# A list scheduler's weights for weights transfers are changed, and the order of a fused GateLoop and SwiGLU kernel is made anew

## The chip, the cores and the metric

The kernel runs on one core of a Trainium2 chip. The time is device microseconds of one execution; the median of three runs before the change is 721.65 us (721.41 to 721.87).

## The reference

Four batches of eight heads run a gated linear recurrence over 768 steps with head size 48. Its result, laid out as 3072 tokens of 384 features, goes through an RMS norm and a SwiGLU feed-forward with 1536 hidden features. The four weights come as 64-bit floats, the rest as 32-bit floats.

```
mag = sqrt(a_re*a_re + a_im*a_im);  scale = minimum(mag, 0.999) / (mag + 1e-06)
for t in range(S):
    new_re = ar * S_re - ai * S_im
    new_im = ar * S_im + ai * S_re
    S_re, S_im = (new_re + einsum('bhd,bhe->bhde', k[t], v[t]), new_im)
    y[t] = einsum('bhd,bhde->bhe', q[t], S_re)
x = y as (batch*time, heads*dim);  xn = x / sqrt(mean(x*x) + 1e-06) * rms_g
g = xn @ w_gate;  out = (g * sigmoid(g) * (xn @ w_val)) @ w_out
```

## The kernel before

**Tiling.** Time is cut into chunks of 128 steps, 24 in all (six for each batch). Gates are computed for units: chunks 0 and 1 alone (units 0 and 1), then pairs. `load_gates` and `load_kq` bring `a_re`, `a_im`, `q` and `k` of a unit; `gates` computes, with products along time on VectorE (`scan`), how much each feature has decayed and turned up to each step, and multiplies `q` and `k` by the cosine and sine of the turn. The results are the rotated rows, `rot`. Six transfers for each chunk move them into the layout by heads, `kq`; in the code they are `moved[n]`, in the profile `kq<-rot`.

`attend(n)` does a chunk: scores (`bank<-kq`, 64 small matmuls whose first operands are parts of `kq`), masking with `COPY_PREDICATED` into `am`, transposes of the keys (`bank<-ident,kq`, copied to `kt` by ScalarE), output (`bank<-am,ve` and `bank<-kq,state`), the new state (`bank<-vn,kt`, then an addition and a product by the decay on VectorE), and the norm: squares on ScalarE (`sq`), their column sum on TensorE (`bank<-ones,sq`), `ssv` on VectorE, the power -0.5 on GpSimd (`rs`, the "root" row), its broadcast over columns (`bank<-ident,rs` for early chunks, through two GpSimd transfers for most later ones), and the normed input `xT` on VectorE.

`feed(g, xT)` does the feed-forward of two chunks. It runs twelve blocks of six matmuls with a moving width of 256, by turns `bank<-xT,wg` and `bank<-xT,wv`; ScalarE takes `Silu` of one into `sg`, and VectorE multiplies by the other into `hT`. Then comes the product with `wo`: for groups 0 and 1 six blocks of four matmuls (`bank<-wo,hT` 128x384), for later groups in a form with seven half-products and sums.

**Weights.** The 64-bit weights are brought in twelve pieces: six of 1536 KB for `w_gate` and `w_val`, and six of 768 KB for `w_out`, all from GpSimd's queue. `fetch` places each raw piece in `wo` or `hT`, which are not needed yet, and after it issues a one-element copy on GpSimd (`junk`) that waits for the landing. From the third piece on a transfer waits for the landing of the one two before it. The last `w_gate` piece (the sixth transfer) is also held until the rows of chunk 1 have landed (`cleared`; the copies `seen` wait for the rows of chunks 0 and 1). The transfers go out in the order 1, 0, 3, 2, 5, 4 of `pieces`, `w_val` ahead of `w_gate`. `narrow` turns a raw piece into 32 bits: an `Activation` on ScalarE, and on VectorE a shift (`TENSOR_SCALAR`), a bit step (`SCALAR_TENSOR_TENSOR`) and an addition (`CUSTOM_DVE_ANT_0`). The same weights are looked at once more later, from SP's queue (`look`), to check their range.

**What sets the order.** Nothing in the loops. Every operation is first recorded by `add` with an assumed duration and, for transfers, an assumed load and packet weight. `dates` goes back from the due times of the feed-forward's blocks to a due time for each operation, and adds `flow.shift[stage, index]`, a table found by a search. `schedule` then plays the list forward: at each moment an engine takes, of its ready operations, the one that is due first. Transfers in flight at once share by their packet weights. `issue` writes the instructions in the order that results. On the chip each engine works strictly in this order and waits on semaphores, so an order that was good under wrong assumptions shows as waiting. SP has eight transfers under way at most: the ninth waits for the first to land. Where the planner sees TensorE idle early on, it puts warm-up matmuls (`bank<-rot` 128x128, `flow.warm`) into the order.

The lines to follow are `dma` (its `load` and `packet`), `flow.shift`, and in the profile line 676, from which all operations are issued, so that groups are told apart by their tiles.

Of the kernel before, what the change touches and what calls it, by code (L numbers as in the profile page):

```python
# [461 lines left out]
class Flow:  # L462
# [9 lines left out]
    turn = 0.0  # L472
# [50 lines left out]
    def add(self, eng, calls, dur, reads=(), writes=(), table=None, land=None, due=None, after=(), behind=(), late=None, mode=None, group=None):  # L523
        op = dict(i=len(self.ops), eng=eng, calls=calls, dur=dur, deps=set(), table=table, land=land,
                  base=due, late=late, mode=mode, group=group, stage=self.stage, behind={o["i"] for o in behind})
        self.ops.append(op)
        op["deps"].update(o["i"] for o in after)
        for ap in reads:
            self.note(op, ap, False)
        for ap in writes:  # L530
            self.note(op, ap, True)
        return op
# [146 lines left out]
def fast(tc, ctx, qT, kT, v, a_re, a_im, w_gate, w_val, w_out, rms_g, out, H, bad):  # L679
# [27 lines left out]
    def room(name, shape, dtype=FP32):  # L707
        t = mem.tile(shape, dtype, name=name, tag=name)
        row = 1
        for x in shape[1:]:  # L710
            row *= x
        rooms[t.tensor.name] = (name, row * mybir.dt.size(dtype))
        keep.append(t)
        return t
# [72 lines left out]
    def run(x):  # L787
        n = 1
        for step, size in reversed([tuple(y) for y in x.ap][0 if x.tensor.name in outside else 1:]):
            if step != n:  # L790
                break
            n *= size
        return n

    def dma(o, x, eng="SP", slow=0.0, **kw):
        n = mybir.dt.size(o.dtype)
        for s in o.shape:
            n *= s
        row = mybir.dt.size(o.dtype) * min(run(o), run(x))
        load = n / row * (0.006 + 50.3e-6 * row) / 16  # L800
        op = add(eng, [(QUEUE[eng].dma_start, (), dict(out=o, in_=x))], 0.85 if eng == "POOL" else 0.62, [x], [o],
                 land=2.0 + 1.4 * load + slow, **kw)
        op["slow"] = slow
        op["load"] = load
        op["packet"] = max(0.07, 0.006 + 50.3e-6 * row * (2 if eng == "POOL" and row == 2048 else 1))
        return op

    def mms(list_, dur, **kw):
# [53 lines left out]
    row = room("row", [P, C])  # L862
# [31 lines left out]
    for o, order in ((band, "p (x h) -> p x h"), (head, "p (x h) -> p h x")):  # L894
        add("DVE", [(nc.vector.tensor_reduce, (), dict(out=o, in_=ident.rearrange(order, h=H), axis=mybir.AxisListType.X,
                                                       op=ALU.add))], 0.3, [ident], [o], late=LATE)
    for r in range(ND):
        o = pick[:, r].rearrange("p (x j) -> p x j", j=2 * ND)[:, :, r::ND]
        copy(o, band.unsqueeze(2).to_broadcast([P, P // H, 2]), late=LATE)
    dma(gcol, rms_g.rearrange("(c p) -> p c", p=P))  # L900


# [21 lines left out]
    def fetch(i, piece, raw, eng):  # L924
        to, ap, c, f = piece
        rows, n = to.shape[1:]
        src = ap.bitcast(I32).rearrange("(c p) f -> p c f", p=P)[:, c, 2 * f:2 * (f + n)]
        raw3 = raw.rearrange("p (c f) -> p c f", c=rows)
        if eng == "POOL" and i >= AHEAD:
            wait = [landed[i - AHEAD]]  # L930
        elif eng == "POOL":
            wait = [begun[0]]
        else:
            wait = []
        if eng == "POOL" and i in CLEAR:
            wait = wait + [cleared[CLEAR[i]]]
        sent = dma(raw3, src, eng, after=wait)
        if eng == "POOL":
            landed[i] = add("POOL", [(nc.gpsimd.tensor_copy, (), dict(out=junk, in_=raw[0:1, 1:2]))], 0.8,
                            after=[sent])  # L940
        words = raw.rearrange("p (n two) -> p n two", two=2)
        return words[:, :, 0], words[:, :, 1]
# [3 lines left out]
    def narrow(i):  # L946
        flow.stage = "w", i
        to, ap, c, f = pieces[i]
        rows, n = to.shape[1:]
        if ap.dtype == FP32:  # L950
            dma(to, ap.rearrange("(c p) f -> p c f", p=P)[:, c, f:f + n], "POOL")
            return
        lo, hi = (x.rearrange("p (c f) -> p c f", f=n) for x in fetch(i, pieces[i], places[i], "POOL"))
        t = to.bitcast(I32)
        act(lo, lo.bitcast(U32), AF.Copy, scale=2.0 ** -29)
        step = n // 2 if i in HALVED else n
        for f in range(0, n, step):
            to_, lo_, hi_ = (x[:, :, f:f + step] for x in (t, lo, hi))
            add("DVE", [(nc.vector.tensor_scalar, (),
                         dict(out=to_, in0=hi_, scalar1=3, scalar2=None, op0=ALU.logical_shift_left))],  # L960
                0.15 + 0.52e-3 * rows * step, [hi_], [to_])
            stt(to_, hi_, 0x3FFFFFFF, to_, ALU.bitwise_or, ALU.bitwise_and)
            tt(to_, to_, lo_, ALU.add)
# [22 lines left out]
    turn = {}  # L986
# [381 lines left out]
    for in_, limit, op in ((ef, P_MIN, ALU.is_ge), (ef, 1.0, ALU.is_le), (range_, 0.0, ALU.is_le),  # L1368
# [15 lines left out]
    flow.warm = dict(after=started, until=WARM, call=[  # L1384
        (nc.tensor.matmul, (banks[3][:, 0:C],), dict(lhsT=filler[:, 0:C], rhs=filler[:, C:2 * C], start=True, stop=True))])
    flow.shift = {
        ("attend", 0): -38.4, ("attend", 1): -1.9, ("attend", 2): -16.2, ("attend", 3): -0.7,
        ("attend", 4): -35.7, ("attend", 6): -12.2, ("attend", 11): -3.9, ("attend", 18): 6.0,
        ("attend", 19): -5.7, ("attend", 20): -1.5, ("attend", 21): 11.1, ("attend", 22): 4.2, ("feed", 4): 7.5,
        ("feed", 7): 1.6, ("feed", 8): 4.4, ("feed", 9): 16.9, ("feed", 11): -26.3, ("kq", 2): -10.9,  # L1390
        ("kq", 6): -3.3, ("kq", 7): -15.8, ("kq", 9): 8.6, ("load", 1): -4.5, ("load", 2): -33.3,
        ("load", 3): 50.7, ("load", 11): -5.2, ("load", 12): -6.8, ("norm", 0): -0.8, ("norm", 1): -5.1,
        ("norm", 5): -4.6, ("norm", 16): 4.4, ("norm", 20): 1.8, ("norm", 21): -20.2, ("norm", 22): -8.0,
        ("root", 1): -1.3, ("root", 2): -5.7, ("root", 3): 41.8, ("root", 5): 2.8, ("root", 9): 9.4,
        ("rot", 1): -4.3, ("rot", 2): 0.4, ("rot", 3): -2.6, ("rot", 5): 10.3, ("rot", 10): -10.2,
        ("rot", 12): 4.7, ("size", 2): -2.7, ("size", 3): 14.9, ("size", 7): -0.3, ("size", 10): 14.6,
        ("size", 11): 53.4, ("size", 12): 18.6, ("state", 0): 20.7, ("state", 1): -6.7, ("state", 2): -18.1,
        ("state", 3): -5.4, ("state", 4): -2.1, ("state", 10): 0.2, ("state", 14): -4.9, ("state", 20): -17.7,
        ("turn", 0): -5.1, ("turn", 1): -18.8, ("turn", 4): 7.1, ("turn", 5): 47.3, ("turn", 6): -2.5,
        ("turn", 8): -28.6, ("turn", 9): 0.3, ("turn", 11): -2.5, ("w", 0): -2.6, ("w", 3): -20.3, ("w", 5): -3.8,  # L1400
        ("w", 6): -7.5, ("w", 10): -31.1, ("y", 0): -12.7, ("y", 1): -1.0, ("y", 7): 1.7, ("y", 10): 4.5,
        ("y", 11): -0.4, ("y", 15): 0.8, ("y", 17): -2.8, ("y", 20): 2.2,
    }
    flow.schedule()
    with tc.manual_schedule():
# [4 lines left out]
def gateloop_swiglu(tc, qT, kT, v, a_re, a_im, w_gate, w_val, w_out, rms_g, out, H):  # L1410
    nc = tc.nc
    with tc.tile_pool(name="flag", bufs=1) as flag:
        bad = flag.tile([1, 1], I32, name="bad")
        with ExitStack() as ctx:
            fast(tc, ctx, qT, kT, v, a_re, a_im, w_gate, w_val, w_out, rms_g, out, H, bad)
        with tc.If(nc.values_load(bad[0:1, 0:1]) > 0):
            general(tc, qT, kT, v, a_re, a_im, w_gate, w_val, w_out, rms_g, out, H)
# [39 lines left out]
```

## Time and profile before

| | |
|---|---|
| median of three runs | 721.65 us |
| profiled execution, its own time | 723.45 us |
| its span (first to last instruction) | 721.7 us |
| TensorE busy | 685.9 us, 95% |
| VectorE, ScalarE, GpSimd busy | 476.2, 328.6, 65.5 us |
| mean granted TensorE clock | 0.991 |
| first feed-forward block starts | 55.81 us |
| chain that ended last: TensorE | 86% |
| DMA queues: SP (q1), GpSimd (q0) | 64.78 MB, 15.35 MB |

In lines by stretch, the numbers after the stretch are its length, and for TensorE, weight loads, VectorE, ScalarE and GpSimd the busy microseconds with the count of instructions; then granted clock, DMA share and GB/s. In a timeline a line has its start, its length, the operation with out<-in, the count, and in brackets the idle time ahead of it with what ended it. One matmul in 32-bit floats leaves two records. In lines of transfers the last number is the median from issue to landing in us.

### The profile page before, as it was taken

To read this page: it belongs to the slowest core of one execution; us is meant where nothing else is said; L and a number is where in the kernel's file an instruction comes from. 1 tells how busy PE (TensorE), PEld (TensorE's weight loads), DVE (VectorE), ACT (ScalarE), POOL (GpSimd) and SP (SyncE) were. 2 spreads that over 40 slices of the span, in tenths; PEclk is the share of its full clock that TensorE was granted. 3 is DMA by queue.
4 is the path that set the end of the run, shared out by engine and by line. 5 is a ranking of instruction groups with operands and counts; after the bars stand their busy time and mean duration, and the time that the engine had idled before them with its cause. 6 is when DMAs were issued, how large, how long until landed. Compare 5 with 4: busy or idle time off the path is not lost.

```text
span 721.7 us, 16275 instructions
## 1 busy us (share of the span) xinstructions
PE 685.9 (95%) x6910; PEld 602.1 (83%) x6910; DVE 476.2 (66%) x756; ACT 328.6 (46%) x448; POOL 65.5 (9%) x106
## 2 busy tenths in 40 slices
PE   0779999999999999999999999999999999999996
PEld 0768877886889889889889889889889889989886
DVE  8998879878788778768757677777553432224121
ACT  8657648866677663837324743735510110010010
POOL 3232100010100001110001001010010000000000
PEclk9988999999999999999999999999999999999999
DMA  9897555535566355463554445444132410020000
GB/s 305 257 279 218 167 147 142 139 97 129 172 151 150 63 131 137 117 173 75 162 111 116 134 106 154 123 90 96 29 75 41 107 7 5 22 56 2 23 1 27
DMA packets 104000, 81.83 MB, mean 113 GB/s; under 512 B 41936, under 2 KB 94416, under 8 KB 103920
## 3 DMA queue, kind: packets, MB, share of 16 engines
q1 hardware_dynamic: 98560, 64.78, 32.8%
q0 software_dynamic: 4416, 15.35, 9.4%
q8 instruction: 56, 0.92, 0.6%
q10 hardware_dynamic: 944, 0.59, 0.3%
q14 instruction: 24, 0.20, 0.1%
HBM read 55.84 MB, written 4.72 MB: 84 GB/s over the span
## 4 chain that ended last, share of the span: by engine, by line
PE 86%; DMA 4%; DVE 4%; ACT 3%; SPq 1%; issue 1%; POOL 0%; DVEq 0%; ACTq 0%; POOLq 0%
PE bank L676 86%; DMA wo<-in_w_val_dram 2%; DMA wo<-in_w_gate_dram 1%; SPq L676 1%; DVE turns L676 1%; ACT turns L676 1%; ACT t L676 1%; ACT L676 1%; DMA in<-in_a_re_dram 1%; DVE rot L676 1%; DVE wv L676 1%; DMA decay<-ends 0%; DVE hT L676 0%; ACT wo L676 0%; POOL rs L676 0%
## 5 line engine op out<-in xcount | busy, mean ns | idle before, releaser
L676 PE MATMUL bank<-xT,wg 128*128 128x256 f32 x864 | 203.5, 386 | 0.0
L676 PE MATMUL bank<-xT,wv 128*128 128x256 f32 x864 | 201.4, 383 | 0.0
L676 PEld LDWEIGHTS bank<-xT,wg 128*128 128x128 f32 x864 | 162.7, 192 | 23.7 <-issue 2.0
L676 PEld LDWEIGHTS bank<-xT,wv 128*128 128x128 f32 x864 | 161.2, 190 | 22.2 <-issue 0.8
L676 ACT ACTIVATE sg<-bank 128x512 f32<-128x512 f32 x72 | 43.0, 597 | 171.1 <-PE bank L676 170.8
L676 DVE TENSOR_TENSOR hT<-bank,sg 128x512 f32<-128x512 f32 x72 | 49.6, 689 | 104.6 <-PE bank L676 99.1
L676 PE MATMUL bank<-wo,hT 128*128 128x192 f32 (+1 forms) x576 | 117.2, 356 | 0.6 <-DVE hT L676 0.5
L676 PEld LDWEIGHTS bank<-wo,hT 128*128 128x128 f32 x576 | 96.0, 190 | 12.3 <-DVE hT L676 1.0
L676 ACT ACT_TABLE_LOAD x64 | 82.1, 1283 | 17.7 <-DVE rot L676 10.2
L676 POOL TENSOR_TENSOR rs<-ssv,mhalf 128x1 f32<-128x1 f32 x24 | 24.8, 1034 | 501.2 <-DVE ssv L676 455.2
L676 DVE TENSOR_TENSOR rot<-kin,turns 128x768 f32<-128x768 f32 x48 | 44.1, 952 | 5.1 <-DMA kq<-rot 4.8
L676 ACT ACTIVATE kt<-bank 128x384 f32<-128x384 f32 x40 | 19.4, 488 | 57.8 <-PE bank L676 55.9
L676 PE MATMUL bank<-sums,hT 128*128 128x192 f32 x240 | 44.3, 327 | 0.0
L676 DVE COPY_PREDICATED am<-causal,bank 128x512 f32<-128x512 int32 x48 | 33.6, 725 | 15.3 <-PE bank L676 15.2
L676 PEld LDWEIGHTS bank<-sums,hT 128*128 128x128 f32 x240 | 39.8, 190 | 0.2
L676 DVE TENSOR_TENSOR hT<-hT 128x768 f32<-128x768 f32 x40 | 38.2, 956 | 0.7
L676 PEld LDWEIGHTS bank<-kq 96*32 96x32 f32 x1536 | 31.0, 112 | 8.8 <-issue 7.6
L676 PE MATMUL bank<-am,ve 128*32 128x128 f32 x768 | 37.3, 275 | 0.0
L676 PE MATMUL bank<-kq 96*32 96x128 f32 (+3 forms) x1536 | 35.4, 240 | 1.1 <-DMA kq<-rot 1.1
L676 ACT ACTIVATE t<-t 128x768 f32<-128x768 f32 (+1 forms) x39 | 30.7, 789 | 8.7 <-DVE t L676 8.3
L676 ACT ACTIVATE turns<-in 128x768 f32<-128x768 f32 (+1 forms) x39 | 30.1, 790 | 8.1 <-DVE in L676 6.1
L676 PE MATMUL bank<-kq,state 96*32 96x128 f32 x640 | 32.5, 272 | 0.2 <-DVE state L676 0.2
(123 smaller groups left out, 727.7 us busy)
## 6 DMA issues: line engine op xcount, KB each, us to landing
kq<-rot SPq DMA_DIRECT2D x144, 128.0 KB, 3.1
kin<-in_q_dram SPq DMA_DIRECT2D x24, 192.0 KB, 3.4
kin<-in_k_dram SPq DMA_DIRECT2D x24, 192.0 KB, 3.5
wo<-in_w_gate_dram SPq DMA_DIRECT2D x6, 768.0 KB, 5.9
wo<-in_w_val_dram SPq DMA_DIRECT2D x6, 768.0 KB, 5.7
wo<-in_w_out_dram SPq DMA_DIRECT2D x6, 768.0 KB, 4.6
out_dram<-ot SPq DMA_DIRECT2D x23, 192.0 KB, 2.3
in<-in_a_re_dram SPq DMA_DIRECT2D x11, 384.0 KB, 4.3
```

What stands on the lines that cost most here:

```text
L676: fn(*args, **kw)
```

## The change

`dma` gives each transfer an assumed load and a packet weight. Before, a transfer from GpSimd's queue had twice the weight if its rows were of 2048 bytes, and the plain weight otherwise; the raw pieces here have rows of 4096 and 3072 bytes, so they had the plain one. After, a transfer from GpSimd's queue with rows over 2048 bytes counts with 0.78 of the load and half the row in its packet weight. All other transfers, the rotated rows among them, keep theirs. The table of stage shifts is a new one with 100 entries in the place of 79.

```diff
-        load = n / row * (0.006 + 50.3e-6 * row) / 16
+        piece = eng == "POOL" and row > 2048
+        load = n / row * (0.006 + 50.3e-6 * row) / 16 * (0.78 if piece else 1.0)
...
-        op["packet"] = max(0.07, 0.006 + 50.3e-6 * row * (2 if eng == "POOL" and row == 2048 else 1))
+        op["packet"] = max(0.07, 0.006 + 50.3e-6 * row * (0.5 if piece else 1.0))
...
     flow.shift = {
-        ("attend", 0): -38.4, ("attend", 1): -1.9, ("attend", 2): -16.2, ("attend", 3): -0.7,
...
-        ("kq", 6): -3.3, ("kq", 7): -15.8, ("kq", 9): 8.6, ("load", 1): -4.5, ("load", 2): -33.3,
-        ("load", 3): 50.7, ("load", 11): -5.2, ("load", 12): -6.8, ("norm", 0): -0.8, ("norm", 1): -5.1,
...
+        ("attend", 0): -38.4, ("attend", 1): -1.9, ("attend", 2): -16.6, ("attend", 3): -1.4,
...
+        ("kq", 2): -47.2, ("kq", 6): -3.3, ("kq", 7): -15.8, ("kq", 8): 0.7, ("kq", 9): 8.6, ("kq", 11): 9.3,
+        ("load", 0): 14.7, ("load", 1): -4.5, ("load", 2): -50.1, ("load", 3): 105.5, ("load", 5): 38.7,
```

What this does to the instructions can only be seen by building both kernels. The orders on the engines differ as follows up to the second group of the feed-forward:

- ScalarE's queue: the second `a_im` load stands after the first table load. GpSimd's first weights transfer waits for this load.
- TensorE: 21 warm-up matmuls ahead of chunk 0's scores (33 before). Half of chunk 1's scores stand ahead of chunk 0's state matmuls and norm column, the other half after them. Chunk 1's state matmuls stand ahead of the first feed-forward (before, after its ninth block).
- TensorE in group 0: twelve gate/value blocks and one output block ahead of chunk 2's scores (before, two output blocks).
- VectorE: chunk 0's masks stand after the first converted piece (before, in the middle of the third), and chunk 0's state addition right after one more shift and one bit step. The last addition of the third `w_val` piece and the first sum of unit 2's gates stand after chunk 1's `xT` (before, ahead of it), and a bit step stands beside chunk 1's root row.
- ScalarE in group 0: one weight conversion, the square of unit 3's `a_re` and the two range checks of unit 2 stand ahead of unit 2's arctangent. The integer copy of the turn stands after the silu of the fifth block pair.
- GpSimd: the fifth weights transfer stands after the first `seen`; the sixth and seventh stand right ahead of chunk 1's root row.
- SP: the first transfer of `look` stands after both chunks' rotated rows, decays and `q`, `k` of the next unit (before, between the rows of chunks 2 and 3).

The last two groups' order on TensorE, from the end of group 9's feed-forward on, is the same in both. From the third chunk on, GpSimd's root rows and their transfers keep their order.

## The prediction

> **What bounds the kernel now.** I read the page's busy table first, then busy time by stretch, then the chain that ended last, then each engine's timeline where the chain leaves TensorE.
>
> ```profile
> PE 685.9 (95%) x6910; PEld 602.1 (83%) x6910; DVE 476.2 (66%) x756; ACT 328.6 (46%) x448; POOL 65.5 (9%) x106
> ...
> 28.00:55.40 27.40, 22.16 (x381) 20.49 (x380) 25.94 (x29) 12.93 (x22) 10.81 (x11) 0.90 0.83 236
> 55.40:87.00 31.60, 31.60 (x181) 27.31 (x181) 28.10 (x38) 22.79 (x27) 5.17 (x10) 0.93 0.62 190
> 87.00:112.00 25.00, 23.41 (x374) 17.46 (x372) 20.92 (x35) 13.97 (x24) 0.98 (x3) 1.00 0.60 167
> ```
>
> TensorE is the bound over the whole, but not at the start. The third column group of the stretches is VectorE: it is busy 25.94 of 27.40 us and 28.10 of 31.60 us, so from 28 to 87 us it idles only 1.46 + 3.50 = 4.96 us. It converts weights and computes gates there, and TensorE waits for what comes out.
>
> ```profile
> 32.98 10.88 DMA wo<-in_w_val_dram
> ...
> 51.88 2.02 POOL rs L676
> ...
> 53.94 22.31 PE bank L676 x92
> ...
> 108.85 444.69 PE bank L676 x4007
> ```
>
> This is the chain: start us, length, what. From 108.85 us on TensorE runs without a break for 445 us, and later breaks sum to about 2 us. A change of order can therefore only move the time by what it does before about 110 us, or by making new breaks afterwards.
>
> ```profile
> 55.81 4.89 PE L676 MATMUL bank<-xT,wg 128*128 128x256 f32 x12
> 60.54 2.75 PE L676 MATMUL bank<-xT,wv 128*128 128x256 f32 x12
> ...
> 92.62 2.74 PE L676 MATMUL bank<-wo,hT 128*128 128x384 f32 x8
> 96.41 1.33 PE L676 MATMUL bank<-kq 96*32 96x128 f32 x64 [1.05 <-DMA kq<-rot]
> ```
>
> The first feed-forward starts at f = 55.81 us. A block (six matmuls, x12 records) takes 2.59 us from start to start; the first takes 4.73. At 96.41 the scores of chunk 2 had waited 1.05 us for the rotated rows. Between lie twelve gate/value blocks, two output blocks and 0.9 us of state: 55.81 + 2.14 + 14 x 2.59 + 0.9 = 95.1 us, as the timeline has it.
>
> **The first part of the change: what stays.** The three cost factors execute nothing. Both kernels issue the same transfers and the same arithmetic, only in other orders; warm-up matmuls fall from 45 to 38, at places where TensorE waits anyway. The 21 ahead of chunk 0 (33 before, 10.5 us) end about 4 us sooner, near 29.4, and TensorE then waits for the rotated rows of chunk 0. These landed at about 31.5 (last issue 26.5, 5.1 to landing). The second a_im load now stands behind the table load on ACT's queue, 1.3 us later, and holds the first weights transfer back as long. It is not first needed before the square of a_re ends near 7.8, so the gates lose nothing; the weights lose up to 1.3 us of a stretch in which the DMA engines are 80 to 100% busy. I take 32.0 for chunk 0 (31.5 to 32.7).
>
> **The second part: a wait between chunk 1's rows and chunk 0's state.** The changed TensorE order puts half of chunk 1's scores ahead of chunk 0's state matmuls, norm column and the rest; VectorE's order puts the state addition ahead of the next weight steps. If the rows of chunk 1 are late, both engines stand.
>
> ```profile
> kq<-rot SPq DMA_DIRECT2D x1, 128.0 KB, 6.6
> ...
> kq<-rot SPq DMA_DIRECT2D x1, 128.0 KB, 2.4
> ...
> kq<-rot SPq DMA_DIRECT2D x1, 128.0 KB, 5.0
> ```
>
> These are issues in narrow windows: the first row set of chunk 0 (issued 23.2, beside a weights transfer), the first of chunk 1 (29.9, alone), and the last of chunk 1 (33.1, just after the fifth weights transfer was issued at 32.98). The last landed at 33.1 + 5.0 = 38.1. Before, that was hidden: its scores ran at 43.04. In the changed order VectorE finishes the first weight piece at 28.0 + 1.68 + 0.87 + 1.67 = 32.2, the fifth transfer goes out near 32.7, and chunk 1's last row near 32.4 to 33.4. If it is caught again it lands at 38.1; alone, by 35. Scores (0.65) and state (0.9) follow: S = 39.7 caught, or 37.3 where the preceding matmuls (to 35.7) decide. VectorE, in its order, has run out at 36.55 (masks done at 34.0, 0.87, 1.68) and idles 3.15 us or 0.75 us. I take caught: a shift of a few tenths either way decides it, and the weights are the ones that move later.
>
> **From there to the feed-forward.** VectorE's list from S, by rows of the timeline: state 0.5, convert 0.87, ssv 0.1, bit step 1.68, two masks 1.24, add 1.67, bit step 1.68, xT 0.5, two adds 3.34, 0.1, convert 0.87, ssv 0.1 = 12.65, so ssv at 52.35. Then a bit step of 1.68 stands on VectorE while GpSimd wants its power. Here a rule can be weighed. The row is 2.02 us at 51.88 beside a VectorE add, against 0.55 for the same power at 665.94 beside nothing. "SBUF — State Buffer", section "SBUF: two separate sides", of the Trainium skill says that a VectorE operation with two SBUF inputs locks the pair of ports against a GpSimd read. The new neighbour has two SBUF inputs, so I take the power as ending 0.5 after it, not 0.55 after ssv; by the shorter row f would be 1.5 us earlier. Column, broadcast and xT add 1.4: f = 56.1 (before 55.81).
>
> **From the feed-forward to chunk 2.** Two pieces of VectorE work (1.67 and 0.87) moved behind xT. ScalarE has a weight conversion (0.83), a square (0.83) and two checks (1.1 with 0.83) put ahead of the arctangent: 3.6 us that before came after it or ahead of the block's silu. The arctangent ends at about f + 21.2 (before 73.85 = f + 18.0). VectorE gets to its scan at 56.05 + 18.9 = 74.95, waits to 77.4 (2.4 us; before 2.79), then 1.95 + 0.47 + 1.8 + 0.9 + 0.5 + 1.85 + 0.5 + 1.77 + 0.9 = 10.6 to the first rotated half: 88.0, against 86.05. The ledger of idle time agrees: 0.5 + 3.15 + 1.3 + 2.4 = 7.35 against 4.96, +2.4 by the one way and +1.95 by the other. I take +2.0. Rows then take what they took, 10.2 us from first issue to last landing: two weights transfers stand 3 to 4 us ahead of them as before (6.9 us for the last). So chunk 2 can start at 98.4.
>
> **What TensorE loses.** It comes there after thirteen blocks, one output block fewer than before: f + 2.14 + 13 x 2.59 = 91.9. It stands 6.5 us, and it still owes the block that used to be done, 2.59 us, after the rows have landed. The end moves by +2.0 + 2.59, less the 0.54 us of small breaks at 106.7 and 108.85, which the extra block covers: +4.05. It can't be won back, since after that TensorE is without slack. Against the span of 721.7 that is 725.75; the profiled execution took 723.45, 1.75 outside the span, and the median of the runs is 721.65, like the span. I say 725.7.
>
> **The clock.** A second rule bears on f.
>
> ```profile
> 52.00:54.00 2.00, 0.36 (x4) 0.17 (x2) 2.00 (x2) 0.00 (x0) 1.89 (x1) 0.82 0.53 94
> 54.00:56.00 2.00, 2.00 (x9) 2.00 (x10) 1.49 (x3) 1.57 (x2) 1.61 (x3) 0.50 0.50 59
> ```
>
> The last three columns are granted clock, DMA share and GB/s. The clock fell to half after 1.64 us of full idleness in a thinly filled stretch. "TensorE: Matmul & The Clock Gate", Part 1, speaks of an idle window of about 3.4 us. By the rule the changed kernel's gaps (about 1 to 2.7 us each) leave the clock whole, the first block takes 2.59 and the arctangent comes 2.1 us sooner, for +2.0 in all; by the row it is half again, +4.05. I take the row.
>
> **The rivals.** (1) Chunk 1's rows escape the fifth transfer: S = 37.3, everything to the first rotated half 2.4 us earlier (85.6), rows at 96.0; the end moves by -0.4 + 2.59 - 0.54 = +1.65: 723.3. For it: the row was 0.13 us from escaping before. Against it: the weights start up to 1.3 us later and hold chunk 0's rows, whose landing releases chunk 1's issues. (2) Faster: chunk 2's rows fly light. Landed alone, as 2.4 us after the last issue, they would be there at 85.7 + 3.8 + 2.4 = 91.9 with rival 1's start, and the end would move by -4.5 + 2.59 - 0.54 = -2.45: 719.2. It decides from a landing before 94.3 on. For it: the two late output-weights transfers are released by VectorE's work and could slip past the rows. Against it: VectorE's order has their release 4 us ahead of the rotation, as now. (3) The second scan stretch is not the end of it: a later group starves by its own reorder, and 3 us more are lost, 729. Before shows none between 112 and 553, so this gets little. (4) The orders change and nothing else: only if the two waits cancel, about 721.7.
>
> **How the numbers follow.** Main case 0.43 (its own range 723.8 to 727.3), rival 1 0.24, faster 0.24, starving 0.05, nothing 0.04. 0.2% is 1.4 us, about what a measurement can tell from no change. Slower by more: 0.40 of the main case, 0.15 of rival 1, the starving 0.05 = 0.60. Faster: 0.22 of the fast case, 0.03 of rival 1 with the full clock = 0.25. The rest, 0.15, is within. The range runs from the fast case's end, 719.4, to the main case with more row sets of chunk 1 caught, 728.5.
>
> **What would show it.** Right: an idle stretch of VectorE of about 3 us ahead of the state near 37 to 40, released by TensorE; f between 55.5 and 57; TensorE idle 4 to 7 us ahead of chunk 2's scores, released by the rotated rows, after thirteen blocks; no new idle time after 115. Wrong: the scores of chunk 1 without a wait; rows of chunk 2 landing less than 8 us after their first issue; the first block at full clock; gaps after 200 us.

## The result, and the profile after

The changed kernel took 731.01 us, the median of four executions (727.21 to 739.22), against 721.60 before (721.41 to 721.87). The ratio is 1.0093, with an interval of 1.0065 to 1.0121: slower by 4.7 to 8.7 us of 721.6. A second series of 22 executions, beside 57 of the kernel before, gave 730.65 us against 723.42 and a ratio of 1.0068 (1.0047 to 1.0089). The ratios leave out executions more than 1.5% above a kernel's fastest, and since the times of the changed kernel spread that far by themselves, its medians lie higher than its ratios (1.3% and 1.0% above the kernel before). The profiled execution took 730.42 us, with a span of 728.7: 7.0 more than the span before.

The first view is the busy table of the changed kernel's page.

```profile
PE 687.6 (94%) x6894; PEld 602.8 (83%) x6894; DVE 474.9 (65%) x756; ACT 330.2 (45%) x449; POOL 63.3 (9%) x106
```

TensorE is busy 1.7 us more than before and the span is 7.0 longer, so most of the loss is TensorE standing. The same three stretches as before, of the changed kernel, say where (busy time of TensorE, its weight loads, VectorE, ScalarE and GpSimd, then granted clock, DMA share, GB/s):

```profile
28.00:55.40 27.40, 19.44 (x342) 17.92 (x341) 18.08 (x18) 10.91 (x15) 3.40 (x6) 0.69 0.72 187
55.40:87.00 31.60, 30.09 (x179) 25.88 (x178) 28.30 (x38) 22.68 (x30) 7.03 (x11) 0.89 0.62 194
87.00:112.00 25.00, 23.14 (x331) 17.85 (x333) 23.17 (x34) 12.85 (x20) 2.74 (x5) 1.00 0.52 160
```

In the first stretch VectorE does 18.08 us of work where it did 25.94, so it idles 9.32 us there and not 1.46. Its timeline has nearly all of that in one place:

```profile
45.00 0.55 DVE L676 TENSOR_TENSOR state<-bank,decay 96x384 f32<-96x384 f32 x1 [7.86 <-PE bank L676]
```

The state addition waits 7.86 us for TensorE, and the weight steps stand behind it. TensorE in its turn waits for rotated rows, as its timeline in the changed kernel shows:

```profile
32.42 1.33 PE L676 MATMUL bank<-kq 96*32 96x128 f32 x64 [2.63 <-DMA kq<-rot]
...
42.38 1.30 PE L676 MATMUL bank<-kq 96*32 96x128 f32 x32 [5.33 <-DMA kq<-rot]
...
61.37 4.65 PE L676 MATMUL bank<-xT,wg 128*128 128x256 f32 x12 [0.29 <-DVE xT L676]
...
99.21 1.33 PE L676 MATMUL bank<-kq 96*32 96x128 f32 x64 [1.80 <-DMA kq<-rot]
...
175.99 1.33 PE L676 MATMUL bank<-kq 96*32 96x128 f32 x64 [1.26 <-DMA kq<-rot]
```

These are the scores of chunks 0, 1, 2 and 6 and, in the middle, the first block of the feed-forward. (With two records for a matmul, x64 is the 32 matmuls of one chunk's scores, and not 64 as the description of the kernel has it.) It starts at f = 61.37, against 55.81. Scores waited for rotated rows four times, 11.0 us in all; before it was once, 1.05. The chain that ended last passes the same places:

```profile
33.60 8.54 DMA kq<-rot
42.38 13.09 PE bank L676 x186
...
57.94 1.87 POOL rs L676
...
61.37 15.02 PE bank L676 x60
...
96.31 2.77 DMA kq<-rot
```

The last row set of chunk 1 was issued at 33.60 and flew 8.54 us.

**A ledger.** The span can be put together from four readings of each trace, relative to the kernel before: (a) the start of chunk 2's scores, less 96.41; (b) 2.59 us for each feed-forward block that before stood ahead of these scores and now stands behind them; (c) idle time of TensorE from these scores to the end, less the 7.42 us of before (0.54 up to 130 us, 6.88 after, most of it the 6.1 us that follow the last matmul); (d) half clock between these scores and 130 us: length times one less the granted clock. For the changed kernel that is 2.80 + 2.59 + (0 + 8.39 - 7.42 = 0.97) + 0 = 6.4 us of the 7.0. Term (b) is put in, not measured; how well the sums fit is its test. The idle part is the new wait at chunk 6, 1.26, less the 0.54 us of small breaks, which the late block covers.

### The profile page after: what moved, and what is told of

Its sections match the earlier page's. It is cut to its first block, busy times and chain, and to the rows that moved or that the text cites. A ratio compares the mean times of both kernels' runs of the same rounds, so it can differ in the third digit from the quotient of the medians.

```text
span 728.7 us, 16231 instructions
## 1 busy us (share of the span) xinstructions
PE 687.6 (94%) x6894; PEld 602.8 (83%) x6894; DVE 474.9 (65%) x756; ACT 330.2 (45%) x449; POOL 63.3 (9%) x106
## 4 chain that ended last, share of the span: by engine, by line
PE 86%; DMA 4%; DVE 3%; ACT 3%; SPq 2%; issue 1%; POOL 0%; DVEq 0%; ACTq 0%
PE bank L676 86%; DMA kq<-rot 4%; SPq L676 2%; DVE turns L676 1%; ACT t L676 1%; DMA in<-in_a_re_dram 1%; DVE wo L676 1%; DVE rot L676 1%; ACT turns L676 0%; ACT in L676 0%; ACT L676 0%; DVE hT L676 0%; POOL rs L676 0%; DVE state L676 0%; ACT wo L676 0%
## 5 line engine op out<-in xcount | busy, mean ns | idle before, releaser
L676 PE MATMUL bank<-kq 96*32 96x96 f32 (+3 forms) x1536 | 35.8, 239 | 11.0 <-DMA kq<-rot 11.0
L676 ACT ACTIVATE t<-in 128x768 f32<-128x768 f32 (+1 forms) x26 | 20.4, 790 | 29.7 <-DVE t L676 8.2
```

The lines of the kernel that those rows point to most:

```text
L676: fn(*args, **kw)
```

## The experiments

The theory in the prediction: TensorE is held before about 110 us and not later; half of chunk 1's scores ahead of chunk 0's state makes TensorE and VectorE wait for chunk 1's rows, and one output block left behind chunk 2's scores is lost time. In the expectations this is theory A. In what follows, rows are "caught" when they fly beside the fifth weights transfer and land late, and they "escape" when they have left ahead of it and land soon; a block is "owed" when it stands behind chunk 2's scores and used to stand ahead of them. Against theory A stood that other parts of the change do it (VectorE's and ScalarE's order, later groups: D), that one half of the diff alone makes it (the costs: C, the dates: T), and that the landing of the rows is no fixed thing of the order (V). Experiments 1 and 2 still call D theory B, and C in experiment 2 means that the loads of the next unit catch the rows. In the diffs, put(x, y) gives x the place just behind y (with a negative last number, just ahead of it), x is taken out of its own place, and no other operation changes its order. The kernel before was measured anew beside each group of runs: 723.44, 722.58 and 723.42 us.

**1. The scores of chunk 1 back behind the state, in the changed kernel.**

```
+    put(ops("PE", "attend", 1)[0], ops("PE", "norm", 0)[0])
```

> The changed kernel with one group of sixteen matmuls moved on TensorE alone: the first half of chunk 1's scores stands behind chunk 0's state matmuls and norm column again. Theory A (that place, with chunk 1's rows caught by the fifth weights transfer): VectorE's idle 7.86 us ahead of chunk 0's state addition falls to about 1.3, the state addition comes at 38.3 instead of 45.0; the rows still land at 42.4, so about 2 us of idle come back ahead of chunk 1's masks; the first feed-forward starts 4.5 to 5 us sooner, at 56.5 to 57, and the time falls by 4.5 us, ratio to before about 1.003. Theory B (the orders of VectorE and ScalarE as a whole cost the time, TensorE's only shows it): the feed-forward starts within 1 us of 61.4, ratio about 1.009 as the changed kernel.

Measured: 728.76 us (726.12 to 730.91), ratio 1.0071 (1.0043 to 1.0099). The feed-forward starts at 57.37, four microseconds sooner than in the changed kernel and nearly where theory A had it. But in this execution the rows also escaped (they flew 2.5 us, see the table below), so the move alone is not shown to be worth these four. And nothing of it arrives at the end:

```profile
98.32 2.24 PE L676 MATMUL bank<-kq 96*32 96x128 f32 x64 [4.92 <-DMA kq<-rot]
```

Chunk 2's scores start 0.9 us sooner, and after the wait of 4.92 us they run at half clock (2.24 us for what takes 1.33). The start is only one of two places that hold the end.

**2. The fifth weights transfer later, in the changed kernel:** GpSimd issues it behind its copy that waits for chunk 1's rows.

```
+    put(ops("POOL", "w", 5)[0], ops("POOL", "rot", 1)[-1])
```

> The changed kernel with one transfer moved on GpSimd alone: the fifth weights transfer stands behind the copy that waits for chunk 1's rows, so it can't fly beside them; all other orders stay. Theory A: the last rows of chunk 1 land near 36 (2.4 us after their issue) instead of 42.4, TensorE's wait of 5.33 us ahead of the first half of the scores vanishes, the state addition comes near 38.6, the feed-forward starts near 55, the weights land near 46 and are not missed before 50; ratio to before 0.999 to 1.002. Theory C (the loads of the next unit on SP's own queue catch the rows as well): rows land after 40, feed-forward after 59, ratio 1.006 or more. Theory B: ratio about 1.009.

Measured: 726.63 us (721.76 to 732.14), ratio 1.0053 (1.0033 to 1.0072). In the trace the transfer goes out at 40.17 rather than 33.04, the last rows of chunk 1 fly 3.9 us, their scores start at 40.00 without a wait, and the feed-forward at 58.19. No expectation held in full: the ratio lies above A's and below C's and B's. One collision is gone, and another has come:

```profile
51.30 0.30 PE L676 MATMUL bank<-am,ve 128*32 128x128 f32 x2 [2.75 <-DMA ve<-in_v_dram]
```

A value transfer of 24 KB that is issued at 41.44 now flies 9.6 us, and chunk 1's output waits for it.

**3. The output block back ahead of chunk 2's scores, in the changed kernel,** with the VectorE addition to its weights.

```
+    put(ops("DVE", "w", 9)[2], ops("DVE", "w", 9)[1])
+    put(ops("PE", "feed", 0)[13], ops("PE", "attend", 2)[0], -0.1)
```

> The changed kernel with the second output block of group 0 put ahead of chunk 2's scores again on TensorE, and with the last addition of the weights that it needs put ahead of the second rotation on VectorE; the start stays as it is. Theory A: the wait of 1.80 us ahead of chunk 2's scores is filled by the block of 2.6, which no longer stands after it: the scores start up to 1 us later, the end comes 1.5 to 1.8 us sooner, ratio about 1.007. If the rows of chunk 2 were not the bound there (VectorE's addition 0.9 us earlier delays chunk 3's rows instead), nothing is gained, ratio about 1.009.

Measured: 729.34 us (728.38 to 736.74), ratio 1.0113 (1.0048 to 1.0178). No gain can be seen, with four executions and a wide interval. Its trace is of use for something else. Of the stretch 32.30 to 33.20 us and the timelines of GpSimd and TensorE:

```profile
kq<-rot SPq DMA_DIRECT2D x2, 128.0 KB, 2.7
```

```profile
33.07 0.78 POOL L676 DMA_DIRECT2D wo<-in_w_val_dram  x1 [0.34 <-issue]
35.24 0.75 POOL L676 COPY seen<-kq 96x1 f32<-96x1 f32 x1 [1.39 <-DMA kq<-rot]
```

Here all rows of chunk 1 were issued (the last at 32.42) before the weights transfer at 33.07. They flew 2.7 us, and the feed-forward started at 56.60, with the scores in their changed place. This is the escape of the prediction's first rival, in one execution. The rival put the feed-forward 2.4 us ahead of 56.1, though, and it came at 56.60.

**4. The scores first, in the kernel before.**

```
+    put(ops("PE", "attend", 1)[0], ops("PE", "state", 0)[2], -0.1)
```

> The kernel before with the first half of chunk 1's scores put ahead of chunk 0's state matmuls, and nothing else: TensorE's order of the changed kernel at this place in the old surroundings. Theory A: the rows land at 38.1 as before, when TensorE comes from chunk 0's outputs at 38.8, so the order costs 0.7 to 1 us of state delay, hidden or not: ratio 1.000 to 1.0015. Theory D (this order is bad by itself, whenever the rows land): the state addition waits several us, ratio over 1.004.

Measured: 729.12 us (721.87 to 734.77), ratio 1.0052 (1.0030 to 1.0073), so by the number it is theory D, and beyond what I had expected of the order alone. TensorE's timeline shows what A had not allowed for, a later landing:

```profile
45.58 1.30 PE L676 MATMUL bank<-kq 96*32 96x128 f32 x32 [5.54 <-DMA kq<-rot]
...
104.85 1.33 PE L676 MATMUL bank<-kq 96*32 96x128 f32 x64 [0.78 <-DMA kq<-rot]
```

In this execution the rows of chunk 1 landed after 45 us; in the trace of the kernel before they had landed at 38.1. There the scores start at 43.04, so a landing up to 43 costs nothing. The single move makes the spread of the times 13 us, against 5 us for the kernel before in the same session.

**5. Both moves undone in the changed kernel** (the edits of 1 and 3 together).

> The changed kernel with both TensorE orders of the start put back at once: the first half of chunk 1's scores behind chunk 0's state matmuls and norm column, and the second output block of group 0 ahead of chunk 2's scores. All is computed. Theory A (two waits in a row: the start is exposed to the landing of chunk 1's rows, and what is won there is lost again at chunk 2's rows as long as an output block that could fill that wait stands behind it): feed-forward from 56.5 to 57.5 us, chunk 2's scores with a wait of 2 to 3 us after fourteen blocks, ratio to the kernel before 1.002 to 1.005, below each of the two edits alone (1.007 and 1.011). Theory D (the rest of the loss has nothing to do with these two places, but with VectorE's order or later groups): ratio 1.006 to 1.010, as with the scores alone. If everything is recovered (ratio under 1.001), these two places are the whole of the loss.

Measured: 730.54 us (726.07 to 735.07, six executions), ratio 1.0107 (1.0074 to 1.0140). Theory A fails here: undoing the two orders doesn't bring the time back. The profiled execution was the fastest of the six. Its ledger is -0.2 + 0 + 0.5 + 1.7 = 2.0 of 2.6 us: chunk 2's scores start as early as before (96.20), and what is left is a wait of 0.94 us at 171.66 and half clock. What made four of the others slower by 4 to 9 us, it can't show.

**6. Half of the diff: new costs, old dates.** This diff and the next are against the changed kernel.

```
-        ("attend", 0): -38.4, ("attend", 1): -1.9, ("attend", 2): -16.6, ("attend", 3): -1.4,
...
+        ("attend", 0): -38.4, ("attend", 1): -1.9, ("attend", 2): -16.2, ("attend", 3): -0.7,
...
```

> Half of the diff: the new cost factors of the transfers with the old table of stage dates. All is computed. TensorE's order here has the first half of chunk 1's scores behind chunk 0's state matmuls, but ahead of its norm column, and chunk 2's scores after thirteen blocks as in the changed kernel. Theory A (what stands behind the landing of chunk 1's rows sets the loss): the state addition doesn't wait, the norm column does, so the feed-forward starts at 57 to 61 us, and the ratio to the kernel before is 1.005 to 1.011. Theory T (the new dates make the loss, the costs alone change nothing that counts): ratio 0.998 to 1.002.

Measured: 726.78 us (721.15 to 732.78), ratio 1.0061 (1.0039 to 1.0083), within the ratios of theory A and outside of T. The start that A gave with it (57 to 61 us) isn't in the trace. The profiled execution was the fastest of twenty, at a span of 719.4, less than that of the kernel before: its rows landed at 37.3, the feed-forward started at 50.97 and the clock stayed whole. In its order the fifth weights transfer goes out only after chunk 1's rows (37.98), and yet the times spread over 12 us. So the collision at that transfer is not the only thing that differs between executions.

**7. The other half: old costs, new dates.**

```
-        load = n / row * (0.006 + 50.3e-6 * row) / 16 * (0.78 if piece else 1.0)
+        load = n / row * (0.006 + 50.3e-6 * row) / 16
...
```

> The other half of the diff: the old cost factors with the new table of stage dates. All is computed. Here chunk 1's scores stand behind chunk 0's norm column, as before, but VectorE's order has the norm of chunk 1 fifteen or so operations later, and TensorE takes chunk 2's scores after ten blocks of the feed-forward rather than fourteen. Theory A: the rows of chunk 1 aren't waited for at the state, yet the feed-forward starts late by VectorE's order, 62 to 68 us, TensorE stands 4 us or more ahead of chunk 2's scores and still owes the output blocks: ratio 1.008 to 1.015. Theory C (the costs make the loss, the dates alone change nothing): ratio 0.998 to 1.002.

Measured: 732.95 us (732.68 to 733.51), ratio 1.0138 (1.0117 to 1.0160), as theory A had it, though not by the wait that it named. The feed-forward starts at 67.14, and TensorE comes to chunk 2's scores at 95.47 after ten blocks, without a wait for them. Four blocks owed, 10.36 us, make the loss: -0.9 + 10.4 - 0.3 = 9.2 of 9.6 us. Costs and dates each lose time alone, so neither half is innocent.

**8. The power of chunk 1's norm set free, in the kernel before.** The VectorE operation beside it goes behind `xT`, and with it the weights transfer that it releases.

```
+    put(ops("DVE", "w", 2)[2], ops("DVE", "norm", 1)[1])
+    put(ops("POOL", "w", 7)[0], ops("DVE", "norm", 1)[1], 0.2)
```

> The kernel before with one VectorE bit step (1.75 us, two SBUF inputs) moved from beside GpSimd's power of chunk 1's norm to behind the normed chunk xT; the output-weights transfer that this bit step releases moves with it, some 3 us later. All is computed. Theory P (the power waits for the neighbouring VectorE operation): the power takes 0.6 to 1.2 us rather than 2.02, the feed-forward starts 0.8 to 1.5 us sooner, and as chunk 2's rotation follows from it, the time is 0.7 to 1.4 us shorter: ratio 0.998 to 0.999. Rival (the landing of chunk 2's rows decides, not the start): the power is shorter, the feed-forward sooner, and the time the same, 0.9993 to 1.001. If the later transfer delays its weights, slower than 1.001.

Measured: 722.02 us (720.76 to 726.17), ratio 0.9993 (0.9980 to 1.0006): the rival's result, no difference that can be told from none. What was moved is the addition of a weight piece, and not a bit step as the expectation has it. VectorE's timeline of the kernel before:

```profile
51.71 1.75 DVE L676 CUSTOM_DVE_ANT_0 wg<-hT,wg 128x3072 uint16<-128x3072 uint16 x1
```

The timelines of GpSimd and VectorE in this run:

```profile
52.66 1.21 POOL L676 TENSOR_TENSOR rs<-ssv,mhalf 128x1 f32<-128x1 f32 x1 [7.01 <-DVE ssv L676]
```

```profile
52.50 0.95 DVE L676 TENSOR_TENSOR t<-t,t 128x768 f32<-128x768 f32 x1
54.52 0.55 DVE L676 TENSOR_TENSOR xT<-yg,bank 128x384 f32<-128x384 f32 x1 [1.08 <-PE bank L676]
```

The power took 1.21 us beside an addition of 0.95, where it took 2.02 beside the weight addition of 1.75: it ends about 0.4 after its neighbour in both. The feed-forward starts at 55.13 rather than 55.81, which doesn't show in the times.

**9. The output block behind, in the kernel before.**

```
+    put(ops("PE", "feed", 0)[13], ops("PE", "state", 2)[0])
```

> The kernel before with one TensorE order of the changed kernel: the second output block of group 0 stands behind chunk 2's scores and their transposes, not ahead of them. All is computed. Theory A (what is owed after the wait is lost time): TensorE comes to the scores 2.59 us sooner, waits 3 to 4 us for the rotated rows rather than 1.05, and does the block then; the end moves by 2.59 less the 0.54 us of small breaks that it covers, +2.05: ratio to the kernel before 1.002 to 1.004. Theory D (chunk 2's rows are so early in most executions that nothing waits): ratio 0.999 to 1.001.

Measured: 724.38 us (720.31 to 731.38), ratio 1.0011 (0.9994 to 1.0028): between the two expectations, and telling neither from the other. In the profiled execution the step costs what was expected and the clock takes more:

```profile
97.11 2.07 PE L676 MATMUL bank<-kq 96*32 96x128 f32 x64 [3.59 <-DMA kq<-rot]
```

```profile
96.00:98.00 2.00, 0.89 (x38) 0.88 0.82 226
98.00:100.00 2.00, 2.00 (x41) 0.50 0.71 200
100.00:102.00 2.00, 2.00 (x6) 0.77 0.12 22
```

The ledger: 0.7 + 2.6 - 0.1 + 1.6 (half clock) = 4.8, against 4.7 measured. The columns here are length, TensorE's busy time, granted clock, DMA share and GB/s.

**10. Both moves, in the kernel before** (the edits of 4 and 9).

> The kernel before with two TensorE orders of the changed kernel: the first half of chunk 1's scores ahead of chunk 0's state matmuls, and the second output block of group 0 behind chunk 2's scores. Every other engine keeps the order of the kernel before. All is computed. Theory A (these two orders on TensorE are the change's loss): ratio to the kernel before 1.007 to 1.010, the sum of 1.005 for the first alone and 1.003 for the second, and a spread of the times as wide as the changed kernel's. Theory D (VectorE's and ScalarE's new order, or later groups, make a part of it): 1.003 to 1.006.

Measured: 727.96 us (722.10 to 734.13), ratio 1.0074 (1.0049 to 1.0098), where the changed kernel had 1.0068 in the same session. The two TensorE orders, put into the old kernel, are enough for a loss of the whole size by the ratios, with nearly the same spread; by the medians of all executions it is 4.5 us against 7.2, so a part may be missing. With experiment 5 this says that they are sufficient for most or all of it, but not what alone has to be undone: the changed order of the other engines has its own way to the same loss.

**11. The scores later, with new costs and old dates** (the edit of 1 in the kernel of 6).

> The new cost factors with the old dates, and the first half of chunk 1's scores put behind chunk 0's norm column on TensorE, so that neither chunk 0's state nor its norm stands behind the rotated rows of chunk 1. All is computed. Theory A (the exposure to those rows makes the loss of this half of the diff, 1.0061): ratio to the kernel before 0.999 to 1.003. Theory D (chunk 2's rows, or this order's thirteen blocks ahead of them, keep it): 1.004 to 1.007. Under 0.999 the order of the other engines would be better than the kernel before.

Measured: 728.38 us (726.11 to 731.67), ratio 1.0077 (1.0048 to 1.0106): just above D's range, and clear of A's. The feed-forward started at 53.81 and chunk 2's scores at 93.19, both sooner than before, and the execution was still 3.8 us longer:

```profile
94.00:96.00 2.00, 2.00 (x36) 0.66 0.37 38
96.00:98.00 2.00, 2.00 (x4) 0.50 0.91 326
...
102.00:104.00 2.00, 0.73 (x20) 1.00 0.11 2
104.00:106.00 2.00, 2.00 (x7) 0.72 0.17 28
106.00:108.00 2.00, 2.00 (x4) 0.50 0.90 259
```

The clock fell to half twice, after waits of 1.77 and 1.27 us. The ledger: -3.2 + 2.6 + 1.0 + 3.3 = 3.7 of 3.8. In the kernel of 6 waits of 1.59 and 1.27 us at the same places left the clock whole.

**12. The changed kernel again.**

> The changed kernel once more, for a second trace and more times. Theory V (the landing of chunk 1's rotated rows differs from execution to execution, and the changed order passes that on): the wait ahead of chunk 1's scores differs from 5.33 us by more than 1 us, the start of the feed-forward moves with it from 61.4, and the times spread over 8 us or more; ratio 1.006 to 1.012. Rival (the landing is a fixed thing of the order): wait within 1 us of 5.33, feed-forward at 60.5 to 62.5, chunk 2's rows and the wait of 1.26 us at chunk 6 as in the first trace.

Measured: 730.65 us (722.21 to 736.80), ratio 1.0068. Theory V holds. The issue of the last row set, with GpSimd's and TensorE's timelines:

```profile
kq<-rot SPq DMA_DIRECT2D x2, 128.0 KB, 11.6
```

```profile
32.53 0.78 POOL L676 DMA_DIRECT2D wo<-in_w_val_dram  x1 [0.40 <-issue]
44.86 0.18 POOL L676 COPY seen<-kq 96x1 f32<-96x1 f32 x1 [11.55 <-DMA kin<-in_k_dram]
```

```profile
44.95 1.29 PE L676 MATMUL bank<-kq 96*32 96x128 f32 x32 [9.84 <-DMA kin<-in_k_dram]
...
62.92 2.86 PE L676 MATMUL bank<-xT,wg 128*128 128x256 f32 x12 [0.71 <-DVE xT L676]
...
99.14 1.33 PE L676 MATMUL bank<-kq 96*32 96x128 f32 x64 [1.72 <-DMA kq<-rot]
```

The wait is 9.84 us rather than 5.33. The profile names another transfer as its end, but the row set itself, issued at 33.05, had 11.6 us of flight and came down just then.

**Caught or not.** Eleven traces have the rows of chunk 1 and the fifth weights transfer close together. "Margin" is the issue of the last row set, less that of the weights transfer, in us.

| kernel | margin | flight of the last set |
|---|---|---|
| 9 output block behind | -1.3 | 2.4 (the sets before it) |
| 10 both moves in the kernel before | -1.2 | 2.4 |
| 3 output block first | -0.65 | 2.7 |
| 1 scores later | -0.5 | 2.5 |
| before | +0.1 | 5.0 |
| 5 both undone | +0.1 | 6.7 |
| 12 changed kernel again | +0.5 | 11.6 |
| changed kernel | +0.6 | 8.5 |
| 4 scores first in the kernel before | +0.6 | 12.0, to the scores |
| 8 power set free | +1.2 | 9.4 |
| 7 old costs, new dates | +2.3 | 9.1 |

Four sets that left first landed within 3 us; seven that left with it or after it took 5 to 12 us. In the other three traces (2, 6 and 11) the transfer was held until the rows had landed, and the last set flew 3.9, 3.8 and 3.4 us. The margin is not a thing of the order: the kernel before, 8 and 9 have the same operations in the same order up to 50 us, and so do 4 and 10, 1 and 5, and the changed kernel, 12 and 3. Each of these four groups has a set that escaped and a set that was caught. A microsecond in issue moves the landing by up to 9 us. Among the caught the margin doesn't give the flight (8.5 and 11.6 us in two executions of one kernel).

What differs between the orders is whether the landing is passed on. In the old order, landings at about 33.7 (experiment 9), 38.1 (before) and 43.1 (8) gave a feed-forward at 57.44, 55.81 and 55.13, with no wait for these rows. In the changed order, landings at 35.0 (3), 42.1 and 44.6 gave 56.60, 61.37 and 62.92.

**From the scores to the end.** The prediction's steps after the landing can be read in the same traces (us):

| kernel | chunk 1's scores | feed-forward f | chunk 2's first row issue | chunk 2's scores |
|---|---|---|---|---|
| before | 43.04 | 55.81 | 86.16 (f + 30.4) | 96.41 (10.2 later) |
| changed | 42.38 | 61.37 (19.0 later) | 93.09 (f + 31.7) | 99.21 (6.1 later) |
| changed, again | 44.95 | 62.92 (18.0 later) | 93.11 (f + 30.2) | 99.14 (6.0 later) |
| 3 output block first | 37.88 | 56.60 (18.7 later) | 88.41 (f + 31.8) | 97.33 (8.9 later) |

In the changed order 18 to 19 us of work stand between chunk 1's scores and the feed-forward; in the old order, 12.8. The ledger's sum stands within 0.9 us of the span's change in twelve of the thirteen new traces, whichever kernel; for the second trace of the changed kernel it is 6.9 of 8.1.

No experiment gave a kernel that is measurably faster than the one before.

## Where the prediction held and where it failed

The direction was right, and the start of its main case, chunk 1's rows caught, is in both traces of the changed kernel. The size was too small: 725.7 forecast (+4.05), 731.0 as median; by the ratio 1.0093 the time is 728.3 (+6.7), by 1.0068 of 723.4 it is +4.9. The top of the range, 728.5, lies just above the first of these and below both medians.

"What stays": held. Chunk 0's rows landed at 32.4 and 31.7 (forecast 32.0).

"A wait between chunk 1's rows and chunk 0's state": right in kind, wrong in one term. The landing was put at 38.1, from a single flight of 5.0 us in the trace of before. It was 42.1 and 44.6: flights of 8.5 and 11.6. VectorE's idle time was 7.86 and not 3.15 us. The landing alone makes 4.0 of the 5.3 us by which f was missed (61.37 against 56.1); the other 1.2 lie between landing and f. Most of that is a term that the prediction left out: behind the wait TensorE's granted clock was 0.50 (42 to 50 us in the first trace), and in both traces the state addition came 2.6 us after the scores began, where 0.65 + 0.9 had been put. The first rival, an escape, is real too, and experiment 3 shows it.

"From there to the feed-forward": held. The forecast had 18.0 us from landing to f; 19.0, 18.0 and 18.7 were measured from the scores. The power took 1.87 us beside the bit step, as forecast, and experiment 8 agrees with the reason. But the 18.0 is luck: in that second trace the power began before the bit step and was short, as the timelines of GpSimd and VectorE show.

```profile
60.51 0.57 POOL L676 TENSOR_TENSOR rs<-ssv,mhalf 128x1 f32<-128x1 f32 x1
```

```profile
60.66 1.75 DVE L676 SCALAR_TENSOR_TENSOR wv<-wo,wv 128x1536 int32<-128x1536 int32 x1
```

The same order gave 0.56 or 0.57 us in the traces of experiments 2, 5 and 12, where the power began first, and 1.86 in those of 1 and 3 and the changed kernel, where the bit step did. So which of the two begins first is open in this order, and the prediction had one case only.

"From the feed-forward to chunk 2": the first half held, the second didn't. The arctangent came at f + 21.2 and the first rotated half issued at f + 31.7, forecast 31.9. In the second trace, with the first block at full clock, it was f + 19.6 and f + 30.2. The flight of the rows was taken as the old 10.2 us and was 6.1: in these executions the two output-weights transfers just ahead landed in 5.0 us (median), against 7.1 in experiment 1, where f was 57.4 and the rows took 9.2. Why they were quicker is open; a late start is not the reason by itself, for experiment 2 has f at 58.19 and rows in 6.2. That gave back 4 of the 5 us lost at f. So two errors of opposite sign, +5.3 and -4.1, met in the sum, and by luck chunk 2's scores came at 99.2, forecast 98.4. Of the signs named beforehand, f between 55.5 and 57 and a wait of 4 to 7 us ahead of these scores failed (61.37, and 1.80 us, since TensorE came there at 97.4 and not 91.9), and one sign of being wrong came true, rows of chunk 2 in less than 8 us. From there to the 7.0 us of the profiled execution it is +0.8 here, 1.26 at chunk 6, 0.25 of other idle time and 0.6 that the ledger leaves unexplained.

"What TensorE loses": with the owed block at 2.59 us, less the 0.54 that it covers, the ledgers of twelve of the thirteen new traces close within 0.9 us. Its forecast of +2.05 for this step is not borne out as a mean: alone in the old kernel it measured 1.0011, or 0.8 us, with an interval that holds zero and ends at 2.0 (1.0028).

"The clock": it goes both ways. The first block ran at half clock in the changed kernel (4.48 us to the next), as the row said, and at full clock in its second trace (2.70), as "TensorE: Matmul & The Clock Gate", Part 1, of the Trainium skill would have it. The same operations stood ahead of it in both, but the waits differed: with the short power a wait of 0.89 us was missing. Neither row nor rule decides it. What I left out is the clock after the wait at chunk 2: up to 3.3 us of the ledger in experiments 3 and 11.

"No new idle time after 115" failed: chunk 6's scores waited 1.26 us at 175.99. The five other traces of the changed order (1, 2, 3, 5 and 12) have a wait of 0.66 to 0.94 us there, and the eight of the old order or of half the diff have none. I had this as a rival with little chance; it is a small part of each loss.

The theory that two orders on TensorE are the loss is half right. They are enough to make it, or most of it (experiment 10), and undoing them isn't enough to remove it (5 and 11). Which operations of the other engines keep the loss, and what differs between executions where the rows aren't caught (6), stays open: a trace is one execution, and those of 5, 6 and 11 were the fastest or among the fastest of their kernels.

## What to carry to other kernels

A transfer that lands late costs nothing as long as its consumer stands late in the queue: before moving that consumer ahead, ask how late the transfer lands in its worst execution, not in the one profiled. Where a small transfer and a large one are issued within a microsecond of each other, treat the landing as having two values, soon or late, and give each a chance. And a wait of 1 to 2 us on TensorE may cost as much again in clock, so a slot that is filled is worth more than its own length.

## What the runs showed of the hardware

A set of 128 KB from SBUF to SBUF flew 2.4 to 2.7 us if it was issued before a weights transfer of 1.5 MB, and 5.0 to 11.6 us if issued 0.1 to 2.3 us after it. With that transfer held back it flew 3.4 to 3.9. Of one kernel, two executions had 8.5 and 11.6.

SP's queue issued the ninth transfer when the first of the nine had landed: in the kernel before, the first row set of chunk 0 (issued 23.16, 6.6 us) landed at 29.8, and the eighth transfer behind it, the first row set of chunk 1, went out at 29.87.

A GpSimd power of one column took 0.55 us beside nothing, and 1.21 to 2.02 us if a VectorE operation of 0.95 to 1.75 us (a shift, a bit step, an addition) had begun just before it; it ended about 0.4 us after that one. Where the power began 0.15 to 0.28 us ahead of the bit step it took 0.56 or 0.57, and the bit step its usual 1.75.

After a wait TensorE's granted clock fell to 0.50 in some executions and not in others. Waits of 1.80 us (changed kernel), 1.72 (12), 1.88 (experiment 10), 1.86 (2), 1.59 and 1.27 (6) left it whole; waits of 1.85 (5), 2.02 (3), 1.77 and 1.27 (11) halved it, and so did those of 3.59 (9) and 4.92 (1). The half clock lasted about 3.3 us, in experiment 3 about 6.7. The stretches of experiment 3:

```profile
96.00:98.00 2.00, 0.67 (x38) 0.99 0.27 79
98.00:100.00 2.00, 2.00 (x44) 0.50 0.69 199
100.00:102.00 2.00, 2.00 (x33) 0.50 0.55 152
102.00:104.00 2.00, 2.00 (x44) 0.50 0.42 93
104.00:106.00 2.00, 2.00 (x90) 0.81 0.08 1
```

Work had resumed at 97.33, so the fall came about 0.6 us after the wait was over. What decides it, none of the runs shows.

The kernel before ranged from 719.15 to 727.88 us over 143 executions on the chips of the three sessions, where its first three had lain within 0.5 us. Three executions were no measure of its spread.
